# Cutting the FFN's chunks of tokens where the attention's batches end

## The chip, the cores and the metric

The kernel runs on one core of a Trainium2 chip. The metric is the time of one execution on the device, in microseconds (us). Times are medians of several executions. All runs in this text are fast, that is, within 1.5% of the fastest of the same kernel. Profiles are of one execution each.

## The reference

An attention with a threshold, then a SwiGLU feed-forward block (FFN), all in float32:

```python
batch, n_heads, seq, head_dim = (8, 8, 576, 64)
scores = scale * np.matmul(q, k.transpose(0, 1, 3, 2))
thresh = np.max(scores, axis=-1, keepdims=True) - tau
scores = np.where(scores >= thresh, scores, -1e9)
attn = softmax(scores)                       # written out in the reference
attn_out = np.matmul(attn, v)
x = attn_out.transpose(0, 2, 1, 3).reshape(8 * 576, 512)
g = x @ w_gate                               # 512 -> 1536
return (silu(g) * (x @ w_val)) @ w_out       # 1536 -> 512
```

A batch has 576 tokens. That is two chunks of 256 and 64 tokens more, and the whole change is about those 64.

## The kernel before

The attention goes pair of heads by pair of heads (a *segment*; four make a batch), and within a segment by five *slots*: four tiles of 128 queries and one of 64. Between the parts of a slot, the program puts pieces of the FFN of tokens whose attention is done. TensorE so has work while VectorE, ScalarE and GpSimd do the softmax. The FFN goes over the 4608 tokens in 18 chunks of 256. A chunk may be cut into *units* where a batch ends inside it, but only for the first two batches:

```python
waiting = deque()
for j in range(NCHUNK):
    ends = [lo for lo in (S - j * TC, 2 * S - j * TC) if 0 < lo < TC]
    waiting.extend((j, lo, hi) for lo, hi in zip([0, *ends], [*ends, TC]))
...
def supply(done):                 # the units that are complete with `done` tokens
    got = []
    while waiting and waiting[0][0] * TC + waiting[0][2] <= done:
        got.append(waiting.popleft())
    return got
```

So chunk 2 is cut into 64 + 192 and chunk 4 into 128 + 128; the others wait until a batch completes them. A unit's hidden layer has 6 pieces each for gate and value (16 matmul records a piece), and the output of each 128 tokens has 4 pieces:

```python
def rows_of_products(j, cs, f, mat, name):
    ...
    for i in range(GR):                       # GR = 2 blocks of 128 features
        for c in range(NCC):                  # 4 blocks of the contraction
            nc.tensor.matmul(ps[:, i], wgv[:, mat, c, (f + i) * P:(f + i + 1) * P], x[:, c, cs],
                             start=(c == 0), stop=(c == NCC - 1))
```

`pace` decides how much FFN a slot gets. It looks at what is ready and at what each later batch will give, and takes the lowest average up to any of those moments, so that work never runs out:

```python
for m in range(...):              # segments ahead
    ...
    if gain:
        r = have / slots
        rate = r if rate is None else min(rate, r)
    have += gain
```

The attention's results are copied from PSUM to the chunks' buffers, with one copy more wherever a batch straddles chunks.

Of the kernel before, what the change touches and what calls it, by code (L numbers as in the profile page):

```python
# [18 lines left out]
def kernel(  # L19
# [24 lines left out]


    nc = tc.nc
    P = 128
# [5 lines left out]
    G = 32  # L53
# [9 lines left out]
    XB = 6  # L63
    NCHUNK = B * S // TC
    NPAIR = B * NP
    TA = 2
    QA = TA * P
    SCALE = 1.0 / float(D) ** 0.5
    assert 2 * D == P and NCC == NP and D == 2 * G and S - SM == 2 * G and B * S % TC == 0

# [36 lines left out]
    TW = 2 * FW  # L107
    spare = const.tile([P, 2 * TW], F32, name="spare")

    XW = NCC * TC  # L110
# [247 lines left out]
    def attend_tile():  # L358

        if not unattended:  # L360
            return
        if not xts:
            start_batch(0)
        seg, t, pT, pT2 = unattended.popleft()
        vr, vr2 = seg["v"]
        n = pT2.shape[1]
        xa = ps_f.tile([P, 512], F32, name="xa", tag="psf")
        for kt in range(KT):
            for h in range(2):
                nc.tensor.matmul(xa[h * D:(h + 1) * D, 0:n], vr[:, h, kt, :], pT[:, h, kt, :],  # L370
                                 start=(kt == 0), stop=False)
        for h in range(2):
            hs = slice(h * D, (h + 1) * D)
            nc.tensor.matmul(xa[hs, 0:n], vr2[hs, :], pT2[hs, :], start=False, stop=True)
        j, lo = divmod(t * P, TC)
        nc.vector.tensor_copy(xts[j].rearrange("p c t a r -> p c (t a r)")[:, seg["i"], lo:lo + n], xa[:, 0:n])

    def attend(seg):

        p, vr, tiles = seg["p"], seg["v"], seg["tiles"]  # L380
        b, cc = divmod(seg["i"], NP)
        tail = NT in tiles
        full = [t for t in tiles if t < NT]
        R = 2
        nj, rows = S // (P // R), P // R
        m = (len(tiles) - tail) * NG // R
        p = p.rearrange("p n (u j q) -> p (n u) j q", u=2, q=G)
        xa = [ps_f.tile([P, 512], F32, name="xa", tag="psf") for _ in range(R)]
        for j in range(nj):
            for a in range(R):  # L390
                rs = slice(a * rows, (a + 1) * rows)
                for h in range(2):


                    n = m + tail
                    lo = n * h
                    at = G - G * (tail and h)
                    nc.tensor.matmul(  # L398
                        xa[a][h * D:(h + 1) * D, at:at + n * G].rearrange("d (i q) -> d i q", q=G),
                        vr[rs, h, j, :], p[rs, lo:lo + n, j, :], start=(j == 0), stop=(j == nj - 1))  # L400
        yield


        first = b * S // (2 * G)
        per = TC // (2 * G)
        puts = deque([nc.vector.tensor_copy, nc.scalar.copy])
        for a in range(R):
            blocks = [first + 2 * t + u for t in full for u in range(2)]
            for j in sorted({x // per for x in blocks}):
                own = [x for x in blocks if x // per == j]  # L410
                i0 = 1 + blocks.index(own[0])
                dst = xts[j][:, cc, own[0] % per:own[-1] % per + 1, a, :]
                puts[0](dst, xa[a][:, i0 * G:(i0 + len(own)) * G].rearrange("d (i q) -> d i q", q=G))  # L413
                puts.rotate(1)
        if tail:
            j, at = divmod(first + SM // (2 * G), per)
            for h in range(2):
                hs = slice(h * D, (h + 1) * D)
                cs = slice((1 + m) * G, (2 + m) * G) if h == 0 else slice(0, G)
                for a in range(2):  # L420
                    puts[0](xts[j][hs, cc, at, a], xa[a][hs, cs])
                    puts.rotate(1)
        yield


# [23 lines left out]
    def gate(j, cs, f, hts, gts):  # L449
        n = cs.stop - cs.start  # L450
        per = rows_per(n)
        if f // 2 not in hts:
            hts[f // 2] = hp.tile([P, 2, TC], F32, name="ht") if j else hfirst[:, f:f + 2, :]
        if f % per == 0:
# [6 lines left out]
    def value(j, cs, f, hts, gts):  # L461
        n = cs.stop - cs.start
        per = rows_per(n)
        ps = rows_of_products(j, cs, f, 1, "pv")
        nc.vector.tensor_tensor(out=hts[f // 2][:, :, cs], in0=gts[f // per][:, f % per:f % per + GR, :], in1=ps,  # L465
                                op=ALU.mult)
        if f % per == per - GR:
            unsig.append((j, gts.pop(f // per), [hts[x][:, :, cs] for x in range((f + GR - per) // 2, f // 2 + 1)]))
        if f == NF - GR and cs.stop == TC:
            del xts[j]  # L470
# [11 lines left out]
    def output(tiles):  # L482
        for j, i in tiles:
            hts = hidden[j]
            po = ps_f.tile([P, 512], F32, name="po", tag="psf")[:, 0:DM]
            for f in range(NF):
                if f % OF == 0:
                    if any(u[0] == j for u in unsig):
                        sigmoids()
                    need(NCC * DFF // FW + DM // ne * (f * P // FW + 1))  # L490
                nc.tensor.matmul(po, hts[f // 2][:, f % 2, i * P:(i + 1) * P], wo[:, f, :],  # L491
                                 start=(f == 0), stop=(f == NF - 1))
                if f == NF - 1:
                    ob = op.tile([P, DM], F32, name="ob")
                    nc.scalar.copy(ob, po)
                    nc.gpsimd.dma_start(out=out[j * TC + i * P:j * TC + (i + 1) * P, :], in_=ob)
                if f % OF == OF - 1:
# [7 lines left out]
    ready = deque()  # L505
    waiting = deque()
    for j in range(NCHUNK):
        ends = [lo for lo in (S - j * TC, 2 * S - j * TC) if 0 < lo < TC]
        waiting.extend((j, lo, hi) for lo, hi in zip([0, *ends], [*ends, TC]))

    def tiles_of(unit):

        j, lo, hi = unit
        return [(c, i) for c in ([0, 1] if j == 1 else [j]) for i in range(TC // P)] if j and hi == TC else []

    def cost(unit):
        return 2 * NF * HCOST * (unit[2] - unit[1]) / TC + len(tiles_of(unit)) * NF / OF * OCOST

    def supply(done):

        got = []
        while waiting and waiting[0][0] * TC + waiting[0][2] <= done:
            got.append(waiting.popleft())
        return got
# [3 lines left out]
    def block():  # L528
        late = iter(())
        while True:  # L530
# [7 lines left out]
            cs = slice(lo, hi)  # L538
            hts, gts = hidden.setdefault(j, {}), {}
            c = GR * HCOST * (hi - lo) / TC  # L540
# [23 lines left out]
    def start_batch(b):  # L564
        for j in range(b * S // TC, ((b + 1) * S - 1) // TC + 1):
            if j not in xts:
                while j - XB in xts:
                    fill(HCOST)
                xts[j] = xall[:, j % XB * XW:(j % XB + 1) * XW].rearrange(
                    "p (c t a r) -> p c t a r", c=NCC, a=2, r=G)  # L570

# [14 lines left out]
    for n, seg in enumerate(segs):  # L586
        done = 0
        if n == NP - 1:
            done = QA
        elif n % NP == NP - 1:  # L590
            done = n // NP * S
        seg["gives"] = supply(done)
        gains.append((len(seg["tiles"]), sum(cost(u) for u in seg["gives"])))
# [145 lines left out]
```

## Time and profile before

| | before |
|---|---|
| median of 3 runs | 1638.61 us (1638.04 to 1640.35) |
| span of the profiled run | 1634.9 us |
| TensorE busy | 1559.3 us (95%) |
| VectorE busy | 1082.5 us (66%) |

The stretches below run from one attention product block to another, which are easy to find in both kernels: the first block of the halved attention (batch 1), the fourth, the twelfth, and the last one. The columns are the stretch, its length, then busy us and count of TensorE's matmuls, of weight loads, VectorE, ScalarE and GpSimd, then the granted clock of TensorE, the DMA share and GB/s. The first view is of the kernel before:

```profile
228.57:359.43 130.86, 120.96 (x1016) 74.86 (x1016) 98.84 (x370) 38.77 (x103) 75.11 (x73) 0.97 0.16 36
359.43:701.84 342.41, 332.35 (x2882) 222.85 (x2881) 262.99 (x953) 129.96 (x306) 187.15 (x191) 1.00 0.16 34
701.84:1420.91 719.07, 712.78 (x5518) 473.63 (x5517) 522.32 (x1870) 261.89 (x594) 380.87 (x369) 1.00 0.14 31
1420.91:1634.90 213.99, 208.41 (x828) 148.18 (x828) 13.32 (x23) 26.15 (x49) 27.08 (x26) 0.99 0.03 10
```

I call them batch 1, batches 2 and 3, batches 4 to 7, and the tail. TensorE idles 9.9 us of 130.9 in the first, 10.1 of 342.4 in the second, 6.3 of 719.1 in the third. The last of these is one wait, where the attention ends. TensorE's timeline there (start, length, instruction, count, and in brackets the idle time before it and who ended it):

```profile
1409.44 5.42 PE L491 MATMUL po<-wo,ht 128*128 128x512 f32 x12
1420.91 6.65 PE L398 MATMUL xa<-p,vall 64*64 64x288 f32 x72 [6.05 <-DVE p L329]
1427.49 15.72 PE L491 MATMUL po<-wo,ht 128*128 128x512 f32 x36
```

### The profile page before, as it was taken

The page shows a single profiled execution, that of the slowest core. Times are in us where ns is not written, and L with a number is a line of the kernel's source. Part 1 is how long each engine was busy: PE and PEld are TensorE (multiplying, and loading weights), DVE is VectorE, ACT ScalarE, POOL GpSimd, SP SyncE. Part 2 cuts the span into 40 slices and gives each one's busy share as a digit, 9 for nine tenths or more (in the row PEclk, how much of TensorE's full clock was granted, in tenths as well). Part 3 has the DMA queues.
Part 4 walks back from the last instruction along what each step waited for, and adds up shares of the span by engine and source line. Part 5 has one row for each costly group of instructions (what it writes and reads, how often), then busy time and mean ns, then how long its engine had stood idle before and what let it go on. Part 6 is the DMA issues. An engine that isn't in the chain of part 4 may idle for free.

```text
span 1634.9 us, 30409 instructions
## 1 busy us (share of the span) xinstructions
PE 1559.3 (95%) x11536; PEld 1048.2 (64%) x11536; DVE 1082.5 (66%) x3648; ACT 611.0 (37%) x1339; POOL 779.3 (48%) x728
## 2 busy tenths in 40 slices
PE   6898779999999999999999999999999999899998
PEld 4575556468565865577575757575756775577865
DVE  6877887877787777777777668776776777500000
ACT  5886543324343342424242434343433243211110
POOL 3554455555555464645555555455545464411111
PEclk9999889999999999999999999999999999999999
DMA  7541221111111111110111111111011110000000
GB/s 170 144 136 59 68 50 30 43 44 30 37 36 37 37 30 43 37 37 16 32 27 43 30 43 30 43 30 43 9 35 30 43 36 23 1 13 7 7 13 13
DMA packets 176352, 66.84 MB, mean 41 GB/s; under 512 B 159568, under 2 KB 159568, under 8 KB 176208
## 3 DMA queue, kind: packets, MB, share of 16 engines
q1 hardware_dynamic: 173328, 55.47, 15.0%
q0 software_dynamic: 2880, 9.44, 1.5%
q8 instruction: 91, 1.49, 0.4%
q14 instruction: 53, 0.43, 0.1%
HBM read 55.44 MB, written 9.44 MB: 40 GB/s over the span
## 4 chain that ended last, share of the span: by engine, by line
PE 76%; DVE 9%; issue 3%; ACT 2%; POOL 2%; DVEq 0%; POOLq 0%; ACTq 0%
PE pg L445 20%; PE po L491 20%; PE pv L445 20%; PE sc L263 8%; PE xa L398 8%; DVE p L303 2%; DVE mx L283 2%; POOL p L315 1%; DVE p L329 1%; DVE mx L240 1%; ACT p L299 1%; ACT L299 1%; POOL ht L476 1%; DVE sums L240 0%; DVE wo L181 0%
## 5 line engine op out<-in xcount | busy, mean ns | idle before, releaser
L315 POOL TENSOR_SCALAR p<-p,ri 128x288 f32<-128x288 f32 x486 | 480.3, 1004 | 515.6 <-DVE ri L311 514.5
L445 PE MATMUL pg<-xall,wgv 128*128 128x256 f32 (+3 forms) x1920 | 408.1, 366 | 5.7 <-POOL wgv L186 5.7
L445 PE MATMUL pv<-xall,wgv 128*128 128x256 f32 (+3 forms) x1920 | 405.1, 364 | 0.0
L445 PEld LDWEIGHTS pg<-xall,wgv 128*128 128x128 f32 x1920 | 339.1, 191 | 74.3 <-issue 21.9
L445 PEld LDWEIGHTS pv<-xall,wgv 128*128 128x128 f32 x1920 | 339.1, 191 | 56.6 <-issue 12.1
L491 PE MATMUL po<-wo,ht 128*128 128x512 f32 x816 | 364.6, 598 | 0.6 <-POOL ht L476 0.6
L303 DVE SCALAR_TENSOR_TENSOR p<-sc,th,p 128x288 f32<-128x288 f32 (+1 forms) x540 | 258.6, 529 | 58.0 <-ACT p L299 56.9
L491 PEld LDWEIGHTS po<-wo,ht 128*128 128x128 f32 x816 | 151.4, 190 | 191.3 <-issue 186.3
L295 ACT ACTIVATE th<-nm,cut 128x4 f32<-128x4 f32 (+1 forms) x140 | 41.6, 297 | 538.4 <-DVE nm L286 538.4
L299 ACT ACTIVATE p<-sc,nm 128x288 f32<-128x288 f32 (+1 forms) x540 | 237.3, 512 | 0.8
L283 DVE TENSOR_REDUCE mx<-sc 128x2 f32<-128x576 f32 x252 | 179.4, 749 | 68.1 <-PE sc L263 67.4
L263 PE MATMUL sc<-kT,qT 64*32 64x288 f32 x4032 | 172.6, 416 | 33.0 <-DVE p L303 32.5
L465 DVE TENSOR_TENSOR ht<-gt,pv 128x512 f32<-128x512 f32 (+3 forms) x114 | 70.3, 620 | 200.6 <-PE pv L445 197.1
L329 DVE STREAM_TRANSPOSE p<-p 128x576 f32<-128x576 f32 x252 | 181.4, 754 | 4.3 <-POOL p L315 4.3
L476 POOL TENSOR_TENSOR ht<-ht,gt 128x512 f32<-128x512 f32 (+3 forms) x114 | 128.8, 1157 | 80.0 <-ACT gt L474 80.0
L263 PEld LDWEIGHTS sc<-kT,qT 64*32 64x32 f32 x4032 | 66.7, 107 | 126.4 <-issue 98.5
L398 PE MATMUL xa<-p,vall 64*64 64x288 f32 x2016 | 133.4, 416 | 10.8 <-DVE p L329 6.1
L398 PEld LDWEIGHTS xa<-p,vall 64*64 64x64 f32 x2016 | 80.5, 137 | 63.9 <-issue 15.6
L459 ACT COPY gt<-pg 128x512 f32<-128x512 f32 (+3 forms) x120 | 65.8, 551 | 145.1 <-PE pg L445 145.0
L413 DVE COPY xall<-xa 128x128 f32<-128x128 f32 (+3 forms) x80 | 17.9, 249 | 128.3 <-PE xa L398 120.2
L240 DVE TENSOR_REDUCE sums<-sums 32x4 f32<-32x4 f32 (+1 forms) x560 | 83.9, 150 | 10.5
L240 DVE TENSOR_REDUCE mx<-mx 32x4 f32<-32x4 f32 (+1 forms) x560 | 83.1, 148 | 10.4
(77 smaller groups left out, 971.0 us busy)
## 6 DMA issues: line engine op xcount, KB each, us to landing
vall<-in_v_dram SPq DMA_DIRECT2D x112, 144.0 KB, 3.2
qraw<-in_q_dram SPq DMA_DIRECT2D x128, 72.0 KB, 2.3
kraw<-in_k_dram SPq DMA_DIRECT2D x128, 72.0 KB, 2.7
out_dram<-ob POOLq DMA_DIRECT2D x36, 256.0 KB, 2.4
wo<-in_moe_w_gate_dram SPq DMA_DIRECT2D x16, 384.0 KB, 3.6
wo<-in_moe_w_val_dram SPq DMA_DIRECT2D x16, 384.0 KB, 4.1
xall<-in_moe_w_out_dram SPq DMA_DIRECT2D x6, 768.0 KB, 5.1
wo<-in_moe_w_out_dram SPq DMA_DIRECT2D x2, 768.0 KB, 4.4
```

Of the source, the lines that this page charges most:

```text
L240: nc.vector.tensor_reduce(out=x[g * G:(g + 1) * G, 0:m, 1], in_=x[o * G:(o + 1) * G, 0:m, 0:1], axis=AX.X, op=ALU.max)
L263: nc.tensor.matmul(ps[g * G:(g + 1) * G, u, 0:SH], qT[hs, col + a * G:col + (a + 1) * G], kT[hs, c * SH:(c + 1) * SH], start=True, stop=True)
L283: nc.vector.tensor_reduce(out=mx[:, 2 * x:2 * x + 2, 0], in_=tile_[:, :, 0:SH], axis=AX.X, op=ALU.max, negate=True)
L299: nc.scalar.activation(ps[x], scs[x], AF.Exp, bias=nm[:, x:x + 1])
L303: nc.vector.scalar_tensor_tensor(out=ps[x], in0=scs[x], scalar=th[:, x:x + 1], in1=ps[x], op0=ALU.is_ge, op1=ALU.mult, accum_out=sm[:, x, ...
L315: nc.gpsimd.tensor_scalar(out=ps[x], in0=ps[x], scalar1=ri[:, x:x + 1], scalar2=None, op0=ALU.mult)
L329: nc.vector.transpose(out=p, in_=p)
L398: nc.tensor.matmul(xa[a][h * D:(h + 1) * D, at:at + n * G].rearrange("d (i q) -> d i q", q=G), vr[rs, h, j, :], p[rs, lo:lo + n, j, :], st ...
L445: nc.tensor.matmul(ps[:, i], wgv[:, mat, c, (f + i) * P:(f + i + 1) * P], x[:, c, cs], start=(c == 0), stop=(c == NCC - 1))
L465: nc.vector.tensor_tensor(out=hts[f // 2][:, :, cs], in0=gts[f // per][:, f % per:f % per + GR, :], in1=ps, op=ALU.mult)
L476: nc.gpsimd.tensor_tensor(out=ht, in0=ht, in1=gt[:, 2 * x:2 * x + 2, :], op=ALU.mult)
L491: nc.tensor.matmul(po, hts[f // 2][:, f % 2, i * P:(i + 1) * P], wo[:, f, :], start=(f == 0), stop=(f == NF - 1))
```

## The change

The intent is that chunks end where batches do. Each batch has two full chunks, and the last 64 tokens of four batches make one chunk more. The first of these two chunks may go in halves, after batch 1 and after batch 3. The core of the diff (evictions, buffers and output addresses are cut):

```diff
-    NCHUNK = B * S // TC
+    NU = SM // TC                 # 2 full chunks of a batch
+    BT = TC // (S - SM)           # 4 batches' last tokens are a chunk
...
-    waiting = deque()
-    for j in range(NCHUNK):
-        ends = [lo for lo in (S - j * TC, 2 * S - j * TC) if 0 < lo < TC]
-        waiting.extend((j, lo, hi) for lo, hi in zip([0, *ends], [*ends, TC]))
...
-    def supply(done):
-        got = []
-        while waiting and waiting[0][0] * TC + waiting[0][2] <= done:
-            got.append(waiting.popleft())
+    def supply(b):
+        got = [(("full", b * NU + u), 0, TC) for u in range(NU)]
+        if b < BT and b % 2:
+            got.append((("last", 0), b // 2 * P, (b // 2 + 1) * P))
+        elif b >= BT and b % BT == BT - 1:
+            got.append((("last", b // BT), 0, TC))
         return got
...
-            for j in sorted({x // per for x in blocks}):     # copies of the attention's results
-                own = [x for x in blocks if x // per == j]
-                ...
+            for u in range(NU):
+                i0 = 1 + u * per
+                puts[0](xts["full", b * NU + u][:, cc, :, a, :], ...)
...
+                    else:                                     # output of last tokens: two transfers a tile
+                        for x in range(2):
+                            at = (j[1] * BT + lo // D + 2 * i + x) * S + SM
+                            nc.gpsimd.dma_start(out=out[at:at + D, :], in_=ob[x * D:(x + 1) * D, :])
```

More of the change, by code (lines that the diff above doesn't have):

```diff
@@ L68 @@
     SCALE = 1.0 / float(D) ** 0.5
-    assert 2 * D == P and NCC == NP and D == 2 * G and S - SM == 2 * G and B * S % TC == 0
+    assert 2 * D == P and NCC == NP and D == 2 * G and S - SM == 2 * G and SM % TC == 0 and B % BT == 0 and QA == TC
     const = ctx.enter_context(tc.tile_pool(name="const", bufs=1))
@@ L374, in attend_tile @@
             nc.tensor.matmul(xa[hs, 0:n], vr2[hs, :], pT2[hs, :], start=False, stop=True)
-        j, lo = divmod(t * P, TC)
-        nc.vector.tensor_copy(xts[j].rearrange("p c t a r -> p c (t a r)")[:, seg["i"], lo:lo + n], xa[:, 0:n])
+        u, lo = divmod(t * P, TC)
+        nc.vector.tensor_copy(xts[("last", 0) if t == NT else ("full", u)].rearrange("p c t a r -> p c (t a r)")[:, seg["i"], lo:lo + n], xa[:, 0:n])
     def attend(seg):
-        p, vr, tiles = seg["p"], seg["v"], seg["tiles"]
+        p, vr = seg["p"], seg["v"]
         b, cc = divmod(seg["i"], NP)
-        tail = NT in tiles
-        full = [t for t in tiles if t < NT]
         R = 2
         nj, rows = S // (P // R), P // R
-        m = (len(tiles) - tail) * NG // R
+        m = NT * NG // R
         p = p.rearrange("p n (u j q) -> p (n u) j q", u=2, q=G)
@@ L392, in attend @@
                 for h in range(2):
-                    n = m + tail
+                    n = m + 1
                     lo = n * h
-                    at = G - G * (tail and h)
+                    at = G - G * h
                     nc.tensor.matmul(
@@ L401, in attend @@
         yield
-        first = b * S // (2 * G)
         per = TC // (2 * G)
@@ L407, in attend @@
         for a in range(R):
-            blocks = [first + 2 * t + u for t in full for u in range(2)]
-            for j in sorted({x // per for x in blocks}):
-                own = [x for x in blocks if x // per == j]
-                i0 = 1 + blocks.index(own[0])
-                dst = xts[j][:, cc, own[0] % per:own[-1] % per + 1, a, :]
-                puts[0](dst, xa[a][:, i0 * G:(i0 + len(own)) * G].rearrange("d (i q) -> d i q", q=G))
-                puts.rotate(1)
-        if tail:
-            j, at = divmod(first + SM // (2 * G), per)
-            for h in range(2):
-                hs = slice(h * D, (h + 1) * D)
-                cs = slice((1 + m) * G, (2 + m) * G) if h == 0 else slice(0, G)
-                for a in range(2):
-                    puts[0](xts[j][hs, cc, at, a], xa[a][hs, cs])
-                    puts.rotate(1)
+            for u in range(NU):
+                i0 = 1 + u * per
+                puts[0](xts["full", b * NU + u][:, cc, :, a, :],
+                        xa[a][:, i0 * G:(i0 + per) * G].rearrange("d (i q) -> d i q", q=G))
+                puts.rotate(1)
+        at = b % BT
+        for h in range(2):
+            hs = slice(h * D, (h + 1) * D)
+            cs = slice((1 + m) * G, (2 + m) * G) if h == 0 else slice(0, G)
+            for a in range(2):
+                puts[0](xts["last", b // BT][hs, cc, at, a], xa[a][hs, cs])
+                puts.rotate(1)
         yield
@@ L452, in gate @@
         if f // 2 not in hts:
-            hts[f // 2] = hp.tile([P, 2, TC], F32, name="ht") if j else hfirst[:, f:f + 2, :]
+            hts[f // 2] = hp.tile([P, 2, TC], F32, name="ht") if j != ("full", 0) else hfirst[:, f:f + 2, :]
         if f % per == 0:
@@ L464, in value @@
         ps = rows_of_products(j, cs, f, 1, "pv")
-        nc.vector.tensor_tensor(out=hts[f // 2][:, :, cs], in0=gts[f // per][:, f % per:f % per + GR, :], in1=ps,
+        nc.vector.tensor_tensor(out=hts[f // 2][:, :, 0:n], in0=gts[f // per][:, f % per:f % per + GR, :], in1=ps,
                                 op=ALU.mult)
         if f % per == per - GR:
-            unsig.append((j, gts.pop(f // per), [hts[x][:, :, cs] for x in range((f + GR - per) // 2, f // 2 + 1)]))
+            unsig.append((hts, gts.pop(f // per), [hts[x][:, :, 0:n] for x in range((f + GR - per) // 2, f // 2 + 1)]))
         if f == NF - GR and cs.stop == TC:
@@ L482, in output @@
     def output(tiles):
-        for j, i in tiles:
-            hts = hidden[j]
+        for (j, lo, hi), i in tiles:
+            hts = hidden[j, lo, hi]
             po = ps_f.tile([P, 512], F32, name="po", tag="psf")[:, 0:DM]
@@ L487, in output @@
                 if f % OF == 0:
-                    if any(u[0] == j for u in unsig):
+                    if any(u[0] is hts for u in unsig):
                         sigmoids()
@@ L495, in output @@
                     nc.scalar.copy(ob, po)
-                    nc.gpsimd.dma_start(out=out[j * TC + i * P:j * TC + (i + 1) * P, :], in_=ob)
+                    kind, at = j
+                    if kind == "full":
+                        b, u = divmod(at, NU)
+                        at = b * S + u * TC + i * P
+                        nc.gpsimd.dma_start(out=out[at:at + P, :], in_=ob)
+                    else:
+                        for x in range(2):
+                            at = (j[1] * BT + lo // D + 2 * i + x) * S + SM
+                            nc.gpsimd.dma_start(out=out[at:at + D, :], in_=ob[x * D:(x + 1) * D, :])
                 if f % OF == OF - 1:
@@ L505 @@
     ready = deque()
-    waiting = deque()
-    for j in range(NCHUNK):
-        ends = [lo for lo in (S - j * TC, 2 * S - j * TC) if 0 < lo < TC]
-        waiting.extend((j, lo, hi) for lo, hi in zip([0, *ends], [*ends, TC]))
     def tiles_of(unit):
-        j, lo, hi = unit
-        return [(c, i) for c in ([0, 1] if j == 1 else [j]) for i in range(TC // P)] if j and hi == TC else []
+        first, second = (("full", 0), 0, TC), (("full", 1), 0, TC)
+        units = [] if unit == first else [first, second] if unit == second else [unit]
+        return [(u, i) for u in units for i in range((u[2] - u[1]) // P)]
     def cost(unit):
         return 2 * NF * HCOST * (unit[2] - unit[1]) / TC + len(tiles_of(unit)) * NF / OF * OCOST
-    def supply(done):
-        got = []
-        while waiting and waiting[0][0] * TC + waiting[0][2] <= done:
-            got.append(waiting.popleft())
+    def supply(b):
[4 more added lines that the diff above has]
+            got.append((("last", b // BT), 0, TC))
         return got
@@ L538, in block @@
             cs = slice(lo, hi)
-            hts, gts = hidden.setdefault(j, {}), {}
+            hts, gts = hidden.setdefault(unit, {}), {}
             c = GR * HCOST * (hi - lo) / TC
@@ L564, in start_batch, with place @@
     def start_batch(b):
-        for j in range(b * S // TC, ((b + 1) * S - 1) // TC + 1):
-            if j not in xts:
-                while j - XB in xts:
-                    fill(HCOST)
-                xts[j] = xall[:, j % XB * XW:(j % XB + 1) * XW].rearrange(
-                    "p (c t a r) -> p c t a r", c=NCC, a=2, r=G)
+        def place(n):
+            return xall[:, n * XW:(n + 1) * XW].rearrange("p (c t a r) -> p c t a r", c=NCC, a=2, r=G)
+        half = XB // 2
+        for u in range(NU):
+            j = b * NU + u
+            while ("full", j - 2 * NU) in xts:
+                fill(HCOST)
+            xts["full", j] = place(b % 2 * half + u)
+        if b % BT == 0:
+            xts["last", b // BT] = place(b // BT % 2 * half + NU)
     arenas = [ptp.tile([P, 2 * NT + 1, S], F32, name="p") for _ in range(2)]
@@ L586 @@
     for n, seg in enumerate(segs):
-        done = 0
+        seg["gives"] = supply(n // NP - 1) if n % NP == NP - 1 and n >= NP else []
         if n == NP - 1:
-            done = QA
-        elif n % NP == NP - 1:
-            done = n // NP * S
-        seg["gives"] = supply(done)
+            seg["gives"] = supply(0)[:1]
+        elif n == 2 * NP - 1:
+            seg["gives"] = supply(0)[1:]
         gains.append((len(seg["tiles"]), sum(cost(u) for u in seg["gives"])))
```

## The prediction

> **What bounds the kernel now.** I read three views in this order: the profile page, the waits of TensorE by stretch, and TensorE's timeline in three places.
>
> The page says that TensorE is busy for 1559.3 of 1634.9 us and that the chain that ended last is 76% TensorE. The slices say when it is not full: up to slice 17 or so, and in the slice in which the attention ends.
>
> ```profile
> span 1634.9 us, 30409 instructions
> PE 1559.3 (95%) x11536; PEld 1048.2 (64%) x11536; DVE 1082.5 (66%) x3648; ACT 611.0 (37%) x1339; POOL 779.3 (48%) x728
> PE   6898779999999999999999999999999999899998
> ...
> PE 76%; DVE 9%; issue 3%; ACT 2%; POOL 2%; DVEq 0%; POOLq 0%; ACTq 0%
> ```
>
> I split the span at the start of batch 1's halved attention (188), where batch 2's second tile begins (359), at batch 4's (747), and at the end of the attention (1421). Columns: stretch, length, then busy time and count of each engine.
>
> ```profile
> 188.00:359.00 171.00, 149.24 (x1205) 94.34 (x1206) 137.83 (x475) 59.15 (x144) 93.86 (x86) 0.94 0.19 44
> 359.00:747.00 388.00, 377.94 (x3261) 257.98 (x3260) 297.12 (x1075) 146.87 (x345) 211.03 (x215) 1.00 0.16 34
> 747.00:1421.00 674.00, 667.71 (x5143) 438.96 (x5145) 488.18 (x1747) 244.98 (x555) 357.13 (x346) 1.00 0.14 31
> 1421.00:1635.00 214.00, 208.32 (x828) 148.09 (x828) 13.32 (x23) 26.15 (x49) 27.08 (x26) 0.99 0.03 10
> ```
>
> TensorE idles 171 - 149.2 = 21.8 us beyond modelled ends in batch 1 (VectorE busy 81%), 10.1 us in batches 2 and 3, and 6.3 us in batches 4 to 7, of which 6.1 is the single wait at the very end of the attention. So batches 4 to 7 and the tail are bound by TensorE's work; batches 2 and 3 nearly; batch 1 only partly. The waits of TensorE in the first two of these stretches have one main name, the scores waiting for VectorE's masking of the tile before (the two score buffers come free there):
>
> ```profile
> PE sc L263 <- DVE p L303: 21.8, 12, 5.9
> PE xa L398 <- ACT gt L474: 4.8, 1, 4.8
> ...
> PE sc L263 <- DVE p L303: 9.4, 9, 3.3
> ```
>
> The timeline shows when that wait bites. Each tile slot of the attention has a scores block and as many pieces of FFN as the pacing gives it:
>
> ```profile
> 282.28 1.20 PE L263 MATMUL sc<-kT,qT 64*32 64x288 f32 x32
> 283.41 5.42 PE L491 MATMUL po<-wo,hfirst 128*128 128x512 f32 x12
> 288.76 1.72 PE L263 MATMUL sc<-kT,qT 64*32 64x288 f32 x32
> 290.41 2.84 PE L491 MATMUL po<-wo,hfirst 128*128 128x512 f32 x6
> 295.17 0.72 PE L263 MATMUL sc<-kT,qT 64*32 64x288 f32 x16 [1.92 <-DVE p L303]
> ```
>
> The slot with two output pieces lasts 288.76 - 282.28 = 6.48 us and has no idle time; the next, with one piece, lasts 295.17 - 288.76 = 6.41 us, of which 1.92 idle. So a slot has a floor of about 6.4 us from the softmax, and FFN work beneath it is free. I use this below.
>
> **What each unit costs.** The profile records each f32 matmul twice. The busy means of the group rows overlap, so I take start to start in the timeline, over runs of 16 records (the next rows begin at 271.46, 505.06, 391.61 and 809.60):
>
> ```profile
> 269.67 1.95 PE L445 MATMUL pv<-xall,wgv 128*128 128x64 f32 x16
> 503.27 1.95 PE L445 MATMUL pg<-xall,wgv 128*128 128x128 f32 x16
> 388.91 2.87 PE L445 MATMUL pv<-xall,wgv 128*128 128x192 f32 x16
> 806.04 3.72 PE L445 MATMUL pg<-xall,wgv 128*128 128x256 f32 x16
> ```
>
> That is 1.79/16 = 112 ns for 64 tokens, 112 ns for 128, 2.70/16 = 169 ns for 192 and 3.56/16 = 222 ns for 256. A 64-token unit costs as much as one of 128.
>
> **What the Trainium skill says.** "TensorE: Matmul & The Clock Gate", section "LDWEIGHTS (loading the stationary operand)", puts a load at columns/1.2 ns, 107 ns for 128 columns, whatever streams past; its section "Back-to-back issue gap" says that the spacing is set by load and matmul together, and that N/2.4 alone is too low at small N. The trace agrees: 64 and 128 tokens both space at 112 ns, near the load's 107, though a load's record lasts 190 ns. "Perfetto Trace Analysis", section "Optimization Strategy", says that a kernel with several regimes may gain by interleaving them; here attention already carries the FFN, and the question is how evenly.
>
> **The change part by part.**
>
> 1. *Units.* The page's groups count 1536, 192, 96 and 96 gate records of 256, 128, 192 and 64 tokens; a unit has 12 x 4 x 2 = 96 of each of gate and value. So before has 16 units of 256, 2 of 128, one of 192 and one of 64. After has 17 of 256 (16 full, and the last tokens of batches 4 to 7) and 2 of 128 (the last tokens of batches 0 and 1, and of 2 and 3). One pair 192 + 64 becomes one 256: 192 records x (112 + 169 - 222) = **11.3 us less TensorE work**. The output matmuls are the same in number.
>
> 2. *Where the work lies.* In the pacing's unit (2 records of 256 tokens, 0.444 us) a full chunk costs 96 for hidden and 48 for output. Batch 0's end gives, for batch 1's 20 slots, chunk 1 with the outputs of two chunks (192) and the 64-token unit (24): 216, that is 10.8 a slot. After, 192 or 9.6 a slot. So the 64-token unit's real 192 x 112 ns = 21.5 us leave batch 1. Later gifts, before: 312, 240, 432, 288, 288, 288; after: 360, 288, 360, 288, 288, 288. The pacing takes the lowest average ahead: before, (312 + 240)/40 = 13.8 a slot in batches 2 and 3, then (432 + 3 x 288)/80 = 16.2; after, 1872/120 = 15.6 throughout. Batch 7 leaves 768 tokens for the tail in both.
>
> 3. *Batch 1.* From the first scores wait to 359 the 21.5 us go out, but not all shows. The segment from 277.75 to 315.58 (37.8 us) is at the floor in every slot already, I give it 1 us. The next, 315.58 to 359.50 (43.9 us), carries most of the 64-token work and can fall to about 37.5: 6.5 us. Before 278 VectorE also joins weights and is the limit: 2 us. Sum **-9.5 us**; the other 12 turn into idle time of TensorE.
>
> 4. *Batches 2 to 7.* 24 units of pacing more: +10.6 us; the 192-token unit's excess over its share, 192 x (169 - 166) ns, goes: -0.6. Idle time: at 13.8 a slot, hidden pieces of 8 come 1.7 to a slot and about a quarter of slots have one; at 15.6, 1.95 and few do. Of the 10 us idle in batches 2 and 3 I expect 7 to go, and about 2 to appear in batches 4 to 7, whose rate falls below 16: -5. Sum **+5 us**.
>
> 5. *Small things.* Evictions of the attention (L413) fall from 80 + 80 to 56 + 56; VectorE loses 19.6 - 56 x 0.285 = 3.6 us, ScalarE about as much, over 28 segments, beside TensorE's work: 0 to -2. Output transfers rise from 36 to 40; one more issue of 0.6 us (L496) lies bare at the end: +0.6.
>
> Sum: -9.5 + 5 + 0.6 - 1 = -5. The two pessimistic choices in 3 (floor, weights) might cost less, so I put it at **-7 us: 1631.5 us**.
>
> **The rivals.**
> - *All of TensorE's saving and the idle time of batches 2 and 3 too.* If batch 1 follows TensorE's work (its segments are only some 5% idle after 269), the time falls by 11 + 7 = 18 us, to 1620. For it: 94% busy. Against: the 6.4 us slots with one piece and with two.
> - *Batch 1 doesn't move at all.* Then 10 us of work appear in later batches that have no room: 1638.6 + 5 = 1644. For it: VectorE at 81% in that stretch. Against: the segment of 43.9 us, which a neighbour beats by 6.
> - *A new wait for buffers.* A unit of 128 now takes six hidden tiles for itself, where 64 + 192 shared six; eight exist. The output of a unit comes after four feature blocks of the next, as before, so I expect none; if it did stall, by its 10.6 us output twice, some 5 to 10 us. Chunk slots are two per batch in turn, and the pacing empties batch b-2 in time.
> - *The split outputs.* Four more transfers of 2.4 us to landing, in a tail where outputs come 10 us apart: hidden but for 0.6 us.
>
> **Range and chances.** The extremes of these are 1620 and 1646; most weight lies between the full saving and none. 8 in 10: 1622 to 1639. 2% is 33 us either way, beyond every rival: faster 0.01, same 0.98, slower 0.01.
>
> **What would show it right or wrong.** No 192- and 64-token records, 1632 of 256 for each of gate and value, 192 of 128 (step 1). TensorE's idle time between 188 and batch 2 rises from 22 us to over 30 while that stretch shortens by 8 to 11 us (step 3); segments of 42.6 us in batches 2 and 3 grow to 44 to 45, those of batches 4 to 7 shrink from 45.6 to about 44.5, all near zero idle (step 4). A wait of the FFN matmuls for hidden tiles or chunk slots, a lower granted clock from the longer idle stretches in batch 1, or slots in batch 1 well under 6.4 us would make the prediction wrong.

## The result

| | before | changed |
|---|---|---|
| median | 1639.25 us (1638.04 to 1640.35, 4 runs) | 1626.00 us (1624.95 to 1627.12, 4 runs) |
| ratio | | 0.9919, 95% interval 0.9902 to 0.9937 |
| span of the profiled run | 1634.9 us | 1625.3 us |
| FFN units | 16 of 256, 2 of 128, 1 of 192, 1 of 64 | 17 of 256, 2 of 128 |

A ratio is the mean time of one kernel's fast runs over that of the other's of the same rounds, so not quite the ratio of the medians. The difference of the medians is 13.25 us, that of the profiled runs 9.6 us. The profiled run of the changed kernel is the slowest of its four, and that of the kernel before (1636.65 us) is faster than its timed runs; 3 us and more between single runs are usual here (e2 and e3 below spread over 7 us).

The page of the changed kernel. TensorE's busy time fell by 10.7 us. Its slices show two eights in batch 1, where nines stood before, and nines from there to the end of the attention:

```profile
span 1625.3 us, 29972 instructions
PE 1548.6 (95%) x11344; PEld 1033.4 (64%) x11344; DVE 1081.0 (67%) x3618; ACT 604.1 (37%) x1304; POOL 780.6 (48%) x726
PE   6898779889999999999999999999999999999998
```

The groups of the changed kernel, by shape (busy us, mean ns): the 64- and 192-token forms are gone.

```profile
L442 PE MATMUL pg<-xall,wgv 128*128 128x256 f32 x1632 | 379.0, 386 | 5.7 <-POOL wgv L190 5.7
L442 PE MATMUL pg<-xall,wgv 128*128 128x128 f32 x192 | 24.0, 278 | 0.0
```

The same four stretches:

```profile
230.50:350.53 120.03, 105.99 (x841) 57.46 (x841) 97.03 (x356) 37.40 (x94) 70.57 (x68) 0.95 0.17 37
350.53:711.20 360.67, 356.26 (x2881) 240.37 (x2881) 267.00 (x956) 131.90 (x299) 194.77 (x191) 1.00 0.15 33
711.20:1414.99 703.79, 697.42 (x5523) 460.91 (x5523) 518.17 (x1853) 255.36 (x577) 378.26 (x370) 1.00 0.14 32
1414.99:1625.30 210.31, 203.88 (x822) 146.60 (x822) 13.25 (x22) 26.02 (x48) 28.14 (x28) 0.99 0.03 11
```

The lead-in, the time up to the first stretch, is 1.9 us longer (230.50 against 228.57; in a second profile of the changed kernel it was 229.11, so this is spread). Batch 1 is shorter by 10.8 us, batches 2 and 3 are longer by 18.3, batches 4 to 7 shorter by 15.3, the tail by 3.7. Idle time of TensorE rises in batch 1 from 9.9 to 14.0 us and falls in batches 2 and 3 from 10.1 to 4.4. The waits of TensorE in the second stretch of the changed kernel (us in total, times, longest):

```profile
PE sc L267 <- DVE p L307: 2.4, 1, 2.4
PE po L488 <- POOL ht L473: 2.0, 1, 2.0
```

The idle column understates what is lost. A matmul's record ends where a model puts it, so a short wait is partly hidden under the record before. Nor does it count the time in which TensorE works at a lower granted clock: at 0.50 it spent 8.6 us of batch 1 and 3.4 us of batches 2 and 3 in the kernel before, 12.8 us and none in the changed kernel. I therefore made a second account. TensorE's *work* in a stretch is its records times the spacing from start to start where it never waits: 222 ns for 256 tokens, 169 for 192, 114 for 128, 112.5 for 64, 441 for an output record, 36 and 63 for the attention's scores and products (the averages of records in batches 4 to 7, or of all records of the form where it is rare). The rest of the stretch is *lost*. From the first matmul to the end of the last, in us (in the tail the spacing is 216 and 431, hence the negative rest):

| stretch | before: length, FFN work, lost | changed: length, FFN work, lost |
|---|---|---|
| up to the first product block of batch 1 | 220.1, 67.5, 145.1 | 221.8, 63.9, 150.4 |
| batch 1 | 130.9, 81.7, 20.0 | 120.0, 63.6, 27.2 |
| batches 2 and 3 | 342.4, 246.1, 18.5 | 360.7, 277.1, 5.9 |
| batches 4 to 7 | 719.1, 558.3, 7.6 | 703.8, 540.2, 10.4 |
| tail | 208.4, 207.3, -3.4 | 203.9, 204.6, -5.3 |
| sum | 1620.9, 1160.9, 187.8 | 1610.2, 1149.4, 188.6 |

So the work fell by 11.5 us, and the lost time stayed: 12.5 us more up to the end of batch 1, 12.6 us less in batches 2 and 3. Two readings fit. In the first, only the saved work matters and the rest is noise between stretches. In the second, the saved work alone would have been lost in batch 1, and the more even supply of work is what kept it. These give different times for a kernel that saves the same work but supplies it unevenly.

### The profile page after: what moved, and what is told of

It reads as the page before. It is cut to its first block, busy times and chain, and to the rows that moved or that the text cites. A ratio compares the mean times of both kernels' runs of the same rounds, so it can differ in the third digit from the quotient of the medians.

```text
span 1625.3 us, 29972 instructions
## 1 busy us (share of the span) xinstructions
PE 1548.6 (95%) x11344; PEld 1033.4 (64%) x11344; DVE 1081.0 (67%) x3618; ACT 604.1 (37%) x1304; POOL 780.6 (48%) x726
## 4 chain that ended last, share of the span: by engine, by line
PE 78%; DVE 9%; POOL 1%; ACT 1%; issue 1%; POOLq 0%; DVEq 0%; ACTq 0%
PE po L488 21%; PE pg L442 21%; PE pv L442 20%; PE sc L267 8%; PE xa L400 8%; DVE p L307 2%; DVE mx L287 2%; DVE p L333 1%; POOL p L319 1%; DVE mx L244 1%; ACT p L303 1%; DVE sums L244 0%; DVE wo L185 0%; ACT L303 0%; POOL ht L473 0%
## 5 line engine op out<-in xcount | busy, mean ns | idle before, releaser
L442 PE MATMUL pg<-xall,wgv 128*128 128x256 f32 (+1 forms) x1824 | 403.0, 374 | 5.7 <-POOL wgv L190 5.7
L442 PE MATMUL pv<-xall,wgv 128*128 128x256 f32 (+1 forms) x1824 | 399.9, 373 | 0.0
L442 PEld LDWEIGHTS pg<-xall,wgv 128*128 128x128 f32 x1824 | 331.4, 192 | 75.7 <-issue 19.2
L442 PEld LDWEIGHTS pv<-xall,wgv 128*128 128x128 f32 x1824 | 331.0, 191 | 60.4 <-issue 11.6
L488 PEld LDWEIGHTS po<-wo,ht 128*128 128x128 f32 x816 | 151.1, 190 | 196.1 <-issue 186.2
L462 DVE TENSOR_TENSOR ht<-gt,pv 128x512 f32<-128x512 f32 (+1 forms) x108 | 69.8, 646 | 191.6 <-PE pv L442 186.3
L473 POOL TENSOR_TENSOR ht<-ht,gt 128x512 f32<-128x512 f32 (+1 forms) x108 | 127.9, 1211 | 80.1 <-ACT gt L471 80.1
L456 ACT COPY gt<-pg 128x512 f32<-128x512 f32 (+1 forms) x114 | 65.0, 570 | 156.6 <-PE pg L442 156.6
L400 PEld LDWEIGHTS xa<-p,vall 64*64 64x64 f32 x2016 | 80.4, 135 | 60.9 <-issue 16.8
L411 DVE COPY xall<-xa 128x128 f32<-128x128 f32 x56 | 13.7, 286 | 115.2 <-PE xa L400 115.2
L244 DVE TENSOR_REDUCE mx<-mx 32x4 f32<-32x4 f32 (+1 forms) x560 | 83.1, 148 | 10.4
```

Of the source, the lines that this page charges most:

```text
L244: nc.vector.tensor_reduce(out=x[g * G:(g + 1) * G, 0:m, 1], in_=x[o * G:(o + 1) * G, 0:m, 0:1], axis=AX.X, op=ALU.max)
L400: nc.tensor.matmul(xa[a][h * D:(h + 1) * D, at:at + n * G].rearrange("d (i q) -> d i q", q=G), vr[rs, h, j, :], p[rs, lo:lo + n, j, :], st ...
L462: nc.vector.tensor_tensor(out=hts[f // 2][:, :, 0:n], in0=gts[f // per][:, f % per:f % per + GR, :], in1=ps, op=ALU.mult)
L473: nc.gpsimd.tensor_tensor(out=ht, in0=ht, in1=gt[:, 2 * x:2 * x + 2, :], op=ALU.mult)
L488: nc.tensor.matmul(po, hts[f // 2][:, f % 2, i * P:(i + 1) * P], wo[:, f, :], start=(f == 0), stop=(f == NF - 1))
```

## The experiments

Kernels of one call ran on the same chip and shared the runs of the kernel before (medians 1637.69, 1638.44, 1638.40 and 1638.67 us in four calls). All gave correct results. Theory A is the second reading (a floor of the softmax in batch 1, and evenness), B the first (TensorE's work), C that the alignment itself (fewer copies, no straddling) gains.

| run | units | supply | median us | ratio to before (95%) |
|---|---|---|---|---|
| changed, again | 17 x 256, 2 x 128 | even | 1625.32 | 0.9923 (0.9909 to 0.9937) |
| e1_join64 | 17 x 256, 2 x 128 | uneven | 1631.90 | 0.9965 (0.9952 to 0.9978) |
| e2_whole | 18 x 256 | uneven | 1635.64 | 0.9991 (0.9977 to 1.0005) |
| e3_after_whole | 18 x 256 | uneven | 1639.46 | 1.0004 (0.9990 to 1.0018) |
| e8_early64 | 17 x 256, 128, 2 x 64 | even | 1639.37 | 1.0009 (0.9995 to 1.0023) |
| e4_pairs64 | before + 4 pairs 64 + 192 | as before | 1684.96 | 1.0289 (1.0274 to 1.0304) |
| e5_pairs128 | before + 4 pairs 128 + 128 | as before | 1644.47 | 1.0038 (1.0021 to 1.0055) |
| e6_floor | as changed | held back from batch 1 | 1691.90 | 1.0327 (1.0312 to 1.0343) |
| e7_fill_end | as changed | even | 1623.65 | 0.9908 (0.9894 to 0.9923) |
| e9_flush | as changed | even | 1620.79 | 0.9889 (0.9874 to 0.9904) |
| e10_fine | as changed | even | 1622.09 | 0.9902 (0.9888 to 0.9916) |
| e11_coarse | as changed | even | 1627.76 | 0.9941 (0.9927 to 0.9955) |

### The saving without the even supply: e1_join64, e2_whole, e3_after_whole

e1 and e2 are the kernel before with fewer cuts; e3 is the changed kernel with its last-token chunk whole.

```diff
 e1  -        ends = [lo for lo in (S - j * TC, 2 * S - j * TC) if 0 < lo < TC]
     +        ends = [lo for lo in (2 * S - j * TC,) if 0 < lo < TC]
 e2  +        ends = []
 e3  -        if b < BT and b % 2:
     -            got.append((("last", 0), b // 2 * P, (b // 2 + 1) * P))
     -        elif b >= BT and b % BT == BT - 1:
     +        if b % BT == BT - 1:
```

> The kernel before, with chunk 2 kept whole (no 64 + 192), nothing else: the same 17 units of 256 and 2 of 128 as the changed kernel, but its uneven supply (14.4 a slot in batches 2 and 3, 16.2 in 4 to 7). Theory A (the softmax floor makes work in batch 1 partly free, and evenness gives the rest): batch 1 shortens by 9 us, the later batches grow by 10 us less some 3 us of idle time, so 1637 us (-1 to -5 us against before). Rival B (only TensorE's records count): -11 us, 1628. Rival C (chunks that end where batches do, with their fewer evictions, are what gains): 0.

> The kernel before with no chunk split at all: 18 units of 256. Theory A and rival B: the same as e1_join64 within 2 us, since 128 + 128 costs 224 ns where 256 costs 222. Rival C: 0 against before.

> The changed kernel with the last tokens of batches 0 to 3 as one unit of 256 at the end of batch 3: units and supply as in e2_whole (14.4 a slot, then 16.2), but aligned with batches. Theory A: 1632 to 1636, slower than the changed kernel by 4 us or more and within 3 us of e2_whole. Rival B: as the changed kernel, 1626. Rival C: 1626, over 8 us faster than e2_whole.

e3 took 1639.46 us, no faster than the kernel before. It has all the saved work and all the alignment. Its batch 1 is as short as in the changed kernel, and its batches 2 and 3 idle 9.8 us as in the kernel before. The second stretch of e3:

```profile
349.47:702.30 352.83, 343.08 (x2690) 221.12 (x2689) 263.22 (x945) 126.89 (x288) 189.73 (x184) 0.99 0.15 34
```

TensorE's waits in it, six for the softmax where the changed kernel has one:

```profile
PE sc L267 <- DVE p L307: 5.3, 6, 1.6
PE po L488 <- POOL ht L473: 4.4, 2, 2.2
```

The account says it in sums: e3 has 1148.3 us of FFN work and 201.2 us lost, of which 27.3 in batch 1 and 19.9 in batches 2 and 3. Against before, 12.6 us of work went and 13.4 us of loss came. e2 is the same without alignment (1148.3 and 200.1), and is within 4 us of e3. Theory B fell: it wanted 1626 to 1628 for all three. C fell too: e3 should have been 8 us faster than e2, and its ratio is the higher one. A had the direction, and underrated the size: it allowed e3 4 us or more against the changed kernel, and it was 14. Its ranges missed e3 (1632 to 1636) and e1 (1 to 5 us below before; it was 5.8). One of e3's six runs took 1632.79 us, the other five 1638.91 to 1640.10; the trace is of the slowest, so what the fast run did differently is open.

Part of e3's loss in batches 2 and 3 is a slower TensorE. The granted clock was 0.50 there in three periods of 3.4 us (from 505.1, 597.3 and 682.6 us), each at or just behind a wait; in the changed kernel it was never below 1.00 in these batches. At half speed 10.2 us cost at most 5.1 us, an estimate, of the 14.0 us by which the two kernels differ there.

e1 missed the claim that 128 + 128 and 256 are the same within 2 us. It is 3.7 us faster than e2. In batches 2 and 3 it loses 11.9 us where e2 loses 16.8. Both have a pace of 14.4 a slot, by the code. The cut chunk gives work earlier, and in pieces of half the length; e11 below tried to tell these apart.

### An even supply without the saving: e8_early64

The changed kernel, but batch 0's last 64 tokens go in batch 1 and batch 1's in batch 2, each as a unit of its own (the bookkeeping of the hidden tiles that they share is cut).

```diff
-        if b < BT and b % 2:
-            got.append((("last", 0), b // 2 * P, (b // 2 + 1) * P))
+        if b == 0:
+            got.append((("last", 0), 0, D))
+        elif b == 1:
+            got.insert(0, (("last", 0), D, P))
+        elif b == 3:
+            got.append((("last", 0), P, TC))
```

> The changed kernel with batch 0's last 64 tokens as a unit of their own in batch 1 and batch 1's last 64 in batch 2 (units of 64, 64, 128 in place of 128, 128): the even supply without the saving of units; 21.5 us more TensorE work than the changed kernel, 10 more than before. The runs so far say that the saving of units alone gains nothing (e2_whole, e3_after_whole) and the supply gains all. If so, the two 64s cost what they leave uncovered: the one in batch 1 some 9 us there, and half of its 21.5 us is given back later; the one in batch 2 another 21.5 for the same nominal work. So 1632 to 1638. If saved TensorE work were what counts in full, 1647.

It took 1639.37 us, 14 us more than the changed kernel, just above the range that theory A gave and well under the 1647 that full cost would give. The account has 21.3 us more FFN work than in the changed kernel (1170.7) and less lost time (178.8 against 186.2 in the changed kernel run beside it). In batch 1 it loses 18.6 us and the changed kernel 26.9: of the 18.1 us of the 64-token unit that lie there (the rest lies in the lead-in), about 8 were free. Against the kernel before, e8 loses 9.0 us less and has 9.8 us more work, since it has two 64-token units where before has one. It is thus no pure test of evenness. That evenness takes loss away fits it, but more filler work could do that too. It does show that buying the supply with 64-token units gives all of the gain back.

### What a pair costs: e4_pairs64 and e5_pairs128

```diff
 e4  +        if 9 <= j < 13:
     +            ends = [D]          # 64 + 192
 e5  +        if 9 <= j < 13:
     +            ends = [P]          # 128 + 128
```

> The kernel before with four more chunks (9 to 12, in the part bound by TensorE) cut into 64 + 192, both parts given at the same moment, so supply and pacing stay. If a pair costs 192 x 59 ns = 11.3 us where TensorE is full: +45 us, 1684 (2.8% slower). If weight loads hide: 0. If the extra is free beneath other work there: under 20 us.

> The same four chunks cut into 128 + 128. If the load of 128 columns sets the floor of 112 ns: 4 x 192 x 2 ns = +1.5 us, so the same within 4 us. If it is the number of units that costs (evictions, sigmoids, switching), as much as e4_pairs64.

e4 is 46.5 us slower than before by the medians, 11.6 us a pair, where 11.3 was worked out. This settles the cost of a 64 + 192 pair where TensorE is full. The busy time of the groups in e4 agrees with a floor beneath 128 tokens (480 records each of 64 and 192):

```profile
L445 PE MATMUL pv<-xall,wgv 128*128 128x192 f32 x480 | 84.2, 329 | 0.0
L445 PE MATMUL pv<-xall,wgv 128*128 128x64 f32 x480 | 58.7, 275 | 0.0
```

58.7/480 is 122 ns of busy time a record of 64 tokens, as much as the 128-token form has in the changed kernel (24.0/192 = 125). e5 is 6 us slower, 1.5 us a pair: more than the expected 0.4, and in sum outside the 4 us that were allowed, since records of 128 tokens space at 114 ns on average and not at the 112 of their best runs (4 x 192 x (2 x 114.5 - 222) ns = 5.4 us). It is not the number of units that costs in e4, for e5 has as many.

### The floor in batch 1: e6_floor

```diff
         elif n == 2 * NP - 1:
-            seg["gives"] = supply(0)[1:]
+            seg["gives"] = []
+        elif n == 3 * NP - 1:
+            seg["gives"] = supply(0)[1:] + supply(1)
```

> The changed kernel with chunk 1 and the first outputs held back from batch 1 to batch 2: the pacing then spreads chunk 0 over batches 0 and 1 at 3 a slot (1.3 us of FFN a slot), and 192 units, 85 us of work, move to batches 2 to 7. Theory A (a softmax floor of some 6.4 us a full slot, 36 to 37 us a segment): batch 1's segments stay at 35 us or more, the stretch shortens by no more than 15 us, batches 2 to 7 grow by 85 us or some of it shifts in batch 0: 1690 or more. Rival (batch 1 is bound by TensorE's work): its segments fall to 25 us or below, and the total stays within 15 us of the changed kernel.

With 17.8 us of FFN work left in batch 1 instead of 63.6, that stretch takes 118.9 us instead of 120.0. Its segments took 42.8, 37.6 and 38.5 us. The shortest is as long as the changed kernel's shortest there. Taking out 45.8 us of work made the stretch 1.1 us shorter, as theory A said. A slot without any FFN in e6 shows the wait:

```profile
262.42 1.20 PE L267 MATMUL sc<-kT,qT 64*32 64x288 f32 x32
268.45 3.04 PE L267 MATMUL sc<-kT,qT 64*32 64x288 f32 x32 [4.83 <-DVE p L307]
```

The whole stretch shows what happened to the clock beside such waits (the last column but two; this window begins and ends 2 us after the product blocks, which start at 215.07 and 334.06):

```profile
217.10:336.00 118.90, 71.96 (x732) 42.84 (x728) 94.06 (x344) 29.78 (x84) 59.13 (x58) 0.73 0.16 31
```

The slot lasts 268.45 - 262.42 = 6.0 us, 4.8 of them idle. But the granted clock is 0.73 in this stretch against 0.95 in the changed kernel, and the next scores take 3.04 us instead of 1.20. The Trainium skill, "TensorE: Matmul & The Clock Gate", section "What's actually happening", says that the clock falls to half after an idle window of some 3.4 us; this trace agrees in kind, with 3.04 us after a wait of 4.83, which is more than twice 1.20. But shorter waits were enough elsewhere: in e3 the granted clock was 0.50 from 505.1 and from 682.6 us, at the end of waits of 2.21 and 2.22 us, while one of 2.40 us in the changed kernel (up to 684.96) left it at 1.00. So e6's floor contains a slower TensorE, and the floor at full clock is lower than its 37.6 us a segment: e10 below has a segment of 35.9 us in batch 1, with 21.2 us of FFN work in it. Also, the lead-in of e6 was 15.5 us shorter than that of the changed kernel, since less of chunk 0 was done there. The lead-in is not free of FFN's cost.

In the changed kernel itself a floor is seen in batch 1's slots, at least with output pieces of this length. Those with two output pieces and with one last as long, 6.5 and 6.3 us:

```profile
317.44 1.20 PE L267 MATMUL sc<-kT,qT 64*32 64x288 f32 x32
318.57 5.42 PE L488 MATMUL po<-wo,ht 128*128 128x512 f32 x12
323.92 1.57 PE L267 MATMUL sc<-kT,qT 64*32 64x288 f32 x32
325.42 2.84 PE L488 MATMUL po<-wo,ht 128*128 128x512 f32 x6
330.19 0.72 PE L267 MATMUL sc<-kT,qT 64*32 64x288 f32 x16 [1.93 <-DVE p L307]
```

### The wait at the end: e7_fill_end

```diff
+    fill(6)                       # one more output piece
     turn(0)
     products = attend(prev)
```

> The changed kernel with one more piece of output work put ahead of the last attention products, where TensorE waited 2.4 us (6.05 us in the kernel before). If that wait sets the end, 2 to 3 us faster than the changed kernel, 1623.5; if something else bounds there, no difference.

The end of the attention in the changed kernel, then in e7:

```profile
1409.77 2.84 PE L488 MATMUL po<-wo,ht 128*128 128x512 f32 x6 [0.83 <-POOL ht L473]
1414.99 4.69 PE L400 MATMUL xa<-p,vall 64*64 64x288 f32 x72 [2.38 <-DVE p L333]
```

```profile
1409.85 5.42 PE L488 MATMUL po<-wo,ht 128*128 128x512 f32 x12 [0.83 <-POOL ht L473]
1415.20 4.60 PE L400 MATMUL xa<-p,vall 64*64 64x288 f32 x72
```

The kernel before waits 6.05 us here; the changed kernel happens to place one output piece more in its last slot and waits 0.83 + 2.38 us. One further piece takes away the rest. The median is 1.7 us below that of the changed kernel in its later call (1625.32) and 2.35 below its first timing. The intervals overlap, so the trace carries this and not the times: the tail is shorter by one piece, 201.2 us against 203.9, and the stretch before it is not longer (703.9 and 703.8).

### Further: e9_flush, e10_fine, e11_coarse

```diff
 e9   (with e7's line)
      +        if f == NF - GR:
      +            sigmoids()        # as soon as a unit's last hidden piece is done
 e10  (with e7's line)
      -    OF = 3
      +    OF = 2                    # output pieces of 2 feature blocks; need() adjusted
 e11  -                yield c       # after gate
      +                if hi - lo > P:
      +                    yield c
      ...
      +                yield c if hi - lo > P else 2 * c
```

> The changed kernel unedited, as the yardstick on the same chip for the three beside it: 0.992 of the kernel before, as when it was first timed.

> The changed kernel with the extra output piece at the end (e7_fill_end) and the sigmoids of a unit sent when its last piece is done. TensorE's three waits for hidden tiles (4.6 us in the changed kernel) should go: 2 to 4 us faster than e7_fill_end, 1620. If the added table loads on ScalarE delay the softmax, slower than e7_fill_end.

> The changed kernel with the extra output piece at the end and output pieces of 2 feature blocks in place of 3. If leftover waits in batches 2 to 7 come from slots that get too little, finer pieces take 1 to 4 us off e7_fill_end: 1621. If each switch costs, slower by up to 3.

> The changed kernel with the pieces of its two 128-token units paired (gate and value together), so that they are as long as those of a full chunk; supply, pace and work stay. e1_join64 was 3.7 us faster than e2_whole with the same pace, perhaps because pieces of half the length fill the slots better. If so, this loses 2 to 5 us against the changed kernel; if the even supply alone saves the idle time, within 1 us of it.

e9 is the fastest kernel: 1620.79 us, ratio 0.9889 against the changed kernel's 0.9923. Against e7 (0.9908) the intervals overlap, so what the sigmoids add rests on the trace, which loses 2.5 us less than e7's from batch 2 to the end of the attention. From batch 2 to the end its trace has one kind of wait on TensorE left, and none for hidden tiles:

```profile
PE sc L267 <- DVE p L307: 4.5, 5, 2.4
```

e10 is not told apart from e7 (0.9902 and 0.9908). Its trace loses 3.9 us less in batch 1 and 4.5 us more in batches 4 to 7, so finer output pieces moved the loss and did not remove it. Its batch 1 takes 116.1 us with the same 63.6 us of FFN work that take 120.0 in the changed kernel, at an equal share of half clock (12.8 us): there the length of the pieces sets the time too, and not the softmax alone. e11 is inconclusive on the length of pieces: 0.9941 against 0.9923 on another chip. That is a loss of 2.4 us by the medians, inside its 2 to 5, but the intervals overlap. Its trace loses 3.1 us more in batches 2 and 3 and 1.7 us less in batches 4 to 7. How much of e1's 3.7 us over e2 comes from shorter pieces, and how much from work that is there earlier, stays open. e11 does settle something else: with the even supply but pieces as long as e3's it is still 10.9 us below the kernel before, where e3 is 1.8 above its own, so most of the gain comes from the supply.

## Why the prediction was right

The prediction was 1631.5 us, 1622 to 1639; the kernel took 1626.0, inside the range and 5.5 us below the centre. The sum had given -5 us; the other 2 of the centre's -7 were judgement. (The upper extreme of 1646 comes from no sum: the highest rival gives 1644.) By its steps:

1. *Units.* Right. The records are as foretold, the saved work is 11.5 us in the account (11.3 was worked out), and e4 measured 11.6 us for a pair.
2. *Where the work lies.* Borne out by what moved: 18.1 us of FFN work left batch 1, 3.6 the lead-in, 18.1 batches 4 to 7, and 31.0 came into batches 2 and 3. The paces themselves are in no view.
3. *Batch 1, -9.5 us.* The sum was right, its parts were not. From the start to the fourth product block the changed kernel is 8.9 us ahead (359.43 - 350.53). The segment foretold at 37.5 us took 350.53 - 312.91 = 37.6. The segment from batch 1's second to third product block was to lose 1 us and grew by 2.6 (40.4 us, before 37.8), though it had 2.6 us less FFN work. In the changed kernel it is thus above a floor of the softmax: e10's finer pieces brought it to 38.1. The one limited by joining weights was to lose 2 and lost 7.2 (42.0, before 49.2). That these errors cancel is luck. Idle time from 188 to 350 us is 162 - 132.9 = 29.1 us, where "over 30" was foretold.
4. *Batches 2 to 7, +5 us.* They grew by 18.3 - 15.3 = 3.0 us. **The term that was mis-sized is the idle time that goes in batches 2 and 3: 7 us were foretold, 12.6 measured.** It was read from the idle column (10 us), which leaves out what the modelled ends hide and the slower clock; the account of work had 18.5 us lost there. (By the idle column alone 5.7 us went.) Batches 4 to 7 gave back 2.8 us, where 2 was foretold. Segments of 45.1 us on average in batches 2 and 3 (360.7/8), and of 44.7 in batches 4 to 7 without the last, which takes 33.1 ((703.8 - 33.1)/15; before 45.7), are close to the 44 to 45 and 44.5 foretold.
5. *Small things, about zero.* The fewer copies can't be seen apart (e2 and e3 differ the other way). The tail was not longer by 0.6 us but shorter by 3.7. One output piece of 2.65 us more lies ahead of the last attention products, in time that was a wait of 6.05 us in the kernel before. The wait also cost more than its length: the product block behind it took 6.58 us at a granted clock of 0.69, and in the changed kernel 4.62 us at 1.00 (the columns are those of the stretches above; first the kernel before):

```profile
1420.91:1427.49 6.58, 6.58 (x73) 4.63 (x73) 0.00 (x0) 0.00 (x0) 0.00 (x0) 0.69 0.01 2
1414.99:1419.61 4.62, 4.62 (x72) 4.18 (x72) 0.00 (x0) 0.00 (x0) 0.00 (x0) 1.00 0.02 4
```

With 0.84 us more from the last matmul's end to the end of the span this is 2.65 + 1.96 - 0.84 = 3.8 us. The sum had no term for the piece or the clock, so this part of the gain is luck. Which pieces the last slot gets follows from the order of all before it, and I had not worked that out.

In the profiles the parts are -8.9 (up to the end of batch 1), +3.0 and -3.7, together -9.6, where the working had -9.5, +5 and about zero. The medians differ by 3.7 us more than these two profiles, which is the spread of single runs. In batches 2 to 7 work rose by 31.0 - 18.1 = 12.9 us (10 foretold, and the piece taken from the tail) and loss fell by 12.6 - 2.8 = 9.8 us (5 foretold).

None of the rivals came true as a whole. "All of TensorE's saving and the idle time too" (1620) failed on batch 1: 18.1 us of FFN work left it, and it became 10.8 us shorter. "Batch 1 doesn't move" (1644) failed by 8.9 us. Of the new waits, one for hidden tiles grew to 4.6 us in three places, and not for want of buffers: the sigmoids were sent late, and e9 took it away. Of the signs that were to speak against the prediction, this wait is one; another, a lower granted clock in batch 1, showed too (0.95, before 0.97). Both were too small to undo the gain. The split outputs stayed hidden but for the last: its two issues take 1.06 us at the end, one took 0.54 before. e3 shows what the prediction did not say: without the even supply the saved work would have gained nothing (five of e3's six runs; the sixth was 5 us below the kernel before).

## What to carry to other kernels

Work taken off the busiest engine is worth less than its size in a stretch where another chain sets the pace: 18.1 us out of batch 1 gave 10.8 here, and 45.8 more in e6 gave 1.1 (there with a slower TensorE). It counts in full only if the remaining work is spread so that the full stretches shrink. A wait can also cost more than its length, through the granted clock. When filler work is woven under another computation, size the gain by stretch, with an account of records times spacing, and check each slot's share against the slot's floor. A matmul unit of 64 columns costs as much as one of 128 here, so collect remainders until they fill 128.

## What the Trainium skill lacked or had wrong

- "TensorE: Matmul & The Clock Gate", section "Back-to-back issue gap", has no spacing for float32. Here each float32 matmul has two records, which space at 222 ns for 256 columns, 169 for 192, 112 for 128 and 112 for 64 (216 for 256 in the tail, without attention between).
- The same page's "LDWEIGHTS (loading the stationary operand)" gives 107 ns for 128 columns. The records of these loads last 190 ns, while the spacing shows about 112: the record of a load is no measure of its cost here, which the page doesn't say.
- "Perfetto Trace Analysis", section "Tensor Engine Instruction (MATMUL, LD_WEIGHTS)", says that ends are estimated. It doesn't say what this does to idle time: 10.1 us of gaps stood for 18.5 us lost in batches 2 and 3, of which at most 1.7 us (an estimate: half of 3.4 us at a clock of 0.50) is the slower clock.
